# Attention and two expert layers on one core: one overflow loop instead of eight, three weight pieces ahead of it, attention's small work reordered

## The chip, the cores and the metric

One core of a Trainium2 chip runs the whole program. A core has five engines that run side by side, each with an instruction queue of its own that it works off in order: PE (matrix multiply; its weight loads are listed as PEld), DVE (vector), ACT (activation), POOL (general) and SP (which here only issues transfers). Transfers issued by SP, ACT and POOL are carried out by 16 DMA engines. Engines wait for each other by semaphores. The metric is the time of one execution in device microseconds.

## The reference

Inputs: q, k, v of 4 x 8 x 576 x 64 (batch, heads, positions, width), all float32, and weights. Three stages:

```
# attention: a coarse one on means of 4 positions, and a local one in a band of +-3 positions
q_d, k_d, v_d = mean over 4 positions of q, k, v
out  = repeat(softmax(q_d k_d^T / 8) v_d, 4) + softmax(band(q k^T / 8)) v
x    = out as (2304 tokens, 512)
# first expert layer: each token goes to one of 8 experts
e    = argmax(x w_gate);  scale = softmax(x w_gate)[e] * sigmoid(x w_output_gate)[e]
y    = scale * (relu(x w1[e]) w2[e])            # w1 (8, 512, 1024), w2 (8, 1024, 512)
# second layer, the same for all tokens
h    = y w_in;  result = (h * cos(h)) w_out     # 512 -> 2048 -> 512
```

## The kernel before

**Attention** (lines 116 to 770). The batches are two halves g of two, the heads four pairs hp: eight units (g, hp) of five items, two coarse (D) and three local (L), 40 items in all. `step(n)` (line 709) lays several items over each other in the order of the program: the scores of item n (`phase_a`, PE, then a maximum on DVE), the exponentials of item n - 1 (ACT) and their division (`phase_s`, two small operations on DVE and a multiplication on POOL, line 379), the transposes of item n - 2 (`phase_b`, PE, copied by ACT) and its product with V (`phase_c`, PE). Beside these stand, for the next unit, the transposes of q and k (`t_chunk`, PE, copied by DVE and ACT) and the sums of four positions (`sums`: q_sum on POOL, k_sum on DVE for units 0 and 1 and else on POOL, v_sum on DVE for unit 0 and else on POOL). SP loads q, k, v of unit u + 2 (`load`, `load_vr`) and the V windows of unit u + 1 (`load_vw`, rows of 70 positions whose unused partitions are zeroed once, lines 195 and 212). There are two V window buffers, `vw[0]` and `vw[1]`.

**The gate of the first half** becomes a list `bg` of small operations once the last tile of unit 3 is there (item 22): 18 operations on DVE, ACT and PE that choose the expert, rank the tokens (`rank`, PE) and give each its place, nine scales of 128 rows, and nine scatters (`scatter_one`, POOL: an indirect transfer of 128 scaled rows to the expert's region `xs` in DRAM). Between them goes `zero_count`, which finds the expert with the most rows so far (`leader`, five steps), and `zero_lead`. `flush(k)` (line 453) runs the list on by k units of cost (scale 2, scatter 4, else 1), twice an item with k = 4. From item 31 on (`early_step`) the weights of that leading expert are loaded, at item 36 its first 144 rows (`early_rows`), and after the items PE computes that expert for these rows. The second half's gate runs in three parts of three tiles behind the last items. `tables` (line 772) then sorts the experts by their number of rows and writes place, rows and the flag `over`: how many have more rows than the capacity CAPS of their place.

**The border** (lines 1097 to 1106). SP loads the first weight piece (`fetch(0)`), then the 408 rows of the largest expert (`load_rows(0)`), then the pieces s = 2 to 5. Then comes `overflow`: each engine loads `over` (line 843) and branches past the body (line 844) where it is 0. The body holds eight loops, one a place, each over that place's rows beyond its capacity in turns of 128; with its loop control it stands eight times in the program. Behind it `part(0)` splits piece 0 into a high and a low part (POOL and DVE), `x_tile(0, j)` transposes the rows (PE), with the high part by ACT and the low part by DVE, and `mm1(0)` needs both. A piece is 512 KB, five fit at a time.

**Experts and second layer** (to line 1266): PE runs matmuls in three passes back to back until the end. The order of all this is the order in which the program is written; there is no planner.

Of the kernel before, what the change touches and what calls it, by code (L numbers as in the profile page):

```python
# [18 lines left out]
NT = B * S  # L19
# [43 lines left out]
class Kernel:  # L63
# [54 lines left out]
    def attention(self, es):  # L118
# [76 lines left out]
        nc.vector.memset(vw[1][64:128], 0.0)  # L195
# [16 lines left out]
        nc.gpsimd.memset(vw[0][64:128], 0.0)  # L212
        nc.gpsimd.memset(vw[0][0:32, 0, 0, :], 0.0)
# [238 lines left out]

        def flush(k, stop=None):
            while bg and k > 0 and bg[0][1].__name__ != stop:
                f = bg.pop(0)[1]
                k -= COST.get(f.__name__, 1) if cur[0] < len(items) else 1
                f()

        def gating(g, i0, n):
# [70 lines left out]
            for t in range(n):  # L530
# [9 lines left out]
                (later if n == TG else scales).append(scatter_one)  # L540
# [168 lines left out]
        def step(n):  # L709
# [5 lines left out]
            if n - 1 in exps:  # L715
                exps.pop(n - 1)()
            if n < len(items):
                phase_a(n)
            evicts = []
# [8 lines left out]
            sums(n)  # L728
# [4 lines left out]
            if 0 <= n - 2 < len(items):  # L733
                phase_b(n - 2)
# [103 lines left out]
    def overflow(self, pool, psum, w1v, w2v):  # L838


        tc, nc = self.tc, self.nc
        ET = mybir.EngineType
        any_over = nc.values_load(self.over, min_val=0, max_val=NE)
        with tc.If(any_over > 0):
# [6 lines left out]
            for r in range(NE):  # L851
                c = CAPS[r]
                nr = nc.values_load(self.tab[0:1, 1, r:r + 1], min_val=0, max_val=NT)
                er = nc.values_load(self.tab[0:1, 0, r:r + 1], engines=[ET.SP], min_val=0, max_val=NE - 1)
                fr = nc.values_load(self.tab[0:1, 2, r:r + 1], engines=[ET.Pool], min_val=0, max_val=NT - EARLY)
                br = nc.values_load(self.tab[0:1, 3, r:r + 1], engines=[ET.SP, ET.Pool], min_val=0, max_val=NE * NT - 128)
                with tc.For_i(c, nr, 128) as i:
                    s = nc.s_assert_within(nr + (c - 128) - i, min_val=0, max_val=NT - 128)
                    col = nc.s_assert_within(fr + s + EARLY, min_val=0, max_val=NT - 128)
                    row = nc.s_assert_within(br + s, min_val=0, max_val=NE * NT - 128)  # L860
                    nc.sync.dma_start(out=x, in_=self.xs[bass.ds(row, 128), 0:DM])
                    for a in range(2):
# [20 lines left out]
    def experts(self, es):  # L883
# [215 lines left out]
        for s in range(2, NWR + 1):  # L1099
            fetch(s)  # L1100
# [181 lines left out]
```

## Time and profile before

| | |
|---|---|
| median of 3 runs | 862.24 us (858.41 to 863.38) |
| the profiled execution | 856.74 us, span 854.8 us from first to last instruction |
| PE busy | 805.5 us (94%), mean granted clock 0.983 |
| DVE, ACT, POOL busy | 525.5, 462.1, 210.6 us |
| attention and gates | to about 204 us of the span |
| experts (first layer) | 207.65 to about 440 us |
| second layer | from there to the end |

In the rows below a line of the timeline is: start in us, duration in us, engine, line of the kernel, operation, output <- inputs, shapes, count, and in brackets how long the engine sat idle before it and what ended that. A "q" behind an engine's name (PEldq, DVEq, SPq) means its sequencer: loads of registers, branches, semaphores and DMA issues. [...]

### The profile page before, as it was taken

To read this page: it belongs to the slowest core of one execution; us is meant where nothing else is said; L and a number is where in the kernel's file an instruction comes from. 1 tells how busy PE (TensorE), PEld (TensorE's weight loads), DVE (VectorE), ACT (ScalarE), POOL (GpSimd) and SP (SyncE) were. 2 spreads that over 40 slices of the span, in tenths; PEclk is the share of its full clock that TensorE was granted. 3 is DMA by queue.
4 is the path that set the end of the run, shared out by engine and by line. 5 is a ranking of instruction groups with operands and counts; after the bars stand their busy time and mean duration, and the time that the engine had idled before them with its cause. 6 is when DMAs were issued, how large, how long until landed. Compare 5 with 4: busy or idle time off the path is not lost.

```text
span 854.8 us, 15523 instructions
## 1 busy us (share of the span) xinstructions
PE 805.5 (94%) x5846; PEld 705.2 (83%) x5846; DVE 525.5 (61%) x952; ACT 462.1 (54%) x1105; POOL 210.6 (25%) x250
## 2 busy tenths in 40 slices
PE   6899987888999999999999989999999999999996
PEld 5778866777999999999986778888888888888895
DVE  4787886673579898997669883434343434343442
ACT  4679787642455655655456564445444444444453
POOL 5587758532000000000038751200020002000100
PEclk9999999989999999999999999999999999999998
DMA  7989959726758989998923320101010001000100
GB/s 150 177 197 235 249 121 252 172 102 229 259 174 221 251 271 237 253 286 251 279 71 99 99 74 1 50 0 50 1 50 0 25 1 46 4 1 1 50 1 25
DMA packets 86570, 107.15 MB, mean 125 GB/s; under 512 B 27837, under 2 KB 59613, under 8 KB 86487
## 3 DMA queue, kind: packets, MB, share of 16 engines
q1 hardware_dynamic: 79455, 85.94, 38.8%
q0 software_dynamic: 4432, 14.86, 4.9%
q10 hardware_dynamic: 2600, 5.27, 2.0%
q8 instruction: 48, 0.79, 0.4%
q14 instruction: 35, 0.29, 0.1%
HBM read 83.88 MB, written 22.19 MB: 124 GB/s over the span
## 4 chain that ended last, share of the span: by engine, by line
PE 60%; issue 7%; DVE 4%; ACT 2%; DMA 2%; POOL 0%; POOLq 0%; ACTq 0%; DVEq 0%; SPq 0%
PE hp L991 10%; PE hp L993 10%; PE hp L992 9%; PE op L993 6%; PE op L991 6%; PE op L992 6%; PE yp L991 4%; PE yp L993 4%; PE yp L992 4%; DMA raw<-in_moe_w_out_dram 2%; PE xp L983 1%; DVE tmp L1062 1%; DVE tmp L1063 1%; ACT w L919 1%; DMA yd<-st 0%
## 5 line engine op out<-in xcount | busy, mean ns | idle before, releaser
L1180 DVE SCALAR_TENSOR_TENSOR n<-n,hp 128x512 f32<-128x512 int32 (+1 forms) x80 | 50.6, 633 | 149.5 <-ACT n L1179 149.5
L1179 ACT ACTIVATE n<-hp 128x512 int32<-128x512 f32 (+1 forms) x80 | 44.3, 554 | 161.1 <-PE hp L993 158.3
L991 PE MATMUL hp<-yh,win 128*128 128x512 f32 (+1 forms) x320 | 118.8, 371 | 0.0
L993 PE MATMUL hp<-yh,win 128*128 128x512 f32 (+1 forms) x320 | 118.6, 371 | 0.0
L992 PE MATMUL hp<-yh,win 128*128 128x512 f32 (+1 forms) x320 | 117.9, 368 | 0.0
L993 PE MATMUL op<-w,g 128*128 128x512 f32 x288 | 114.2, 397 | 3.1 <-DVE g L920 3.0
L991 PE MATMUL op<-w,g 128*128 128x512 f32 x288 | 113.9, 396 | 2.2 <-ACT g L919 2.2
L992 PE MATMUL op<-w,g 128*128 128x512 f32 x288 | 113.7, 395 | 0.0
L1212 POOL DMA_INDIRECT out_dram<-o,ids_sb x18 | 18.7, 1038 | 310.1 <-DVE o L1210 306.2
L920 DVE TENSOR_TENSOR w<-wr,w 128x1024 fp32r<-128x1024 f32 x64 | 78.2, 1222 | 21.5 <-ACT w L919 16.5
L1187 DVE SCALAR_TENSOR_TENSOR n<-n,hp 128x512 f32<-128x512 f32 (+1 forms) x80 | 50.7, 633 | 52.9 <-ACT n L1186 52.9
L991 PE MATMUL yp<-h,w 128*128 128x408 f32 (+7 forms) x256 | 78.1, 305 | 2.5 <-DVE st L1027 2.4
L993 PE MATMUL yp<-h,w 128*128 128x408 f32 (+7 forms) x256 | 77.7, 303 | 0.0
L991 PE MATMUL hp<-xt,w 128*128 128x344 f32 (+7 forms) x252 | 77.6, 308 | 0.0
L992 PE MATMUL yp<-h,w 128*128 128x408 f32 (+7 forms) x256 | 77.6, 303 | 0.0
L993 PE MATMUL hp<-xt,w 128*128 128x344 f32 (+7 forms) x252 | 76.1, 302 | 0.0
L992 PE MATMUL hp<-xt,w 128*128 128x344 f32 (+7 forms) x252 | 76.0, 301 | 0.0
L1010 ACT ACTIVATE h<-hp 128x408 fp32r<-128x408 f32 (+7 forms) x64 | 27.2, 425 | 84.0 <-PE hp L993 81.1
L992 PEld LDWEIGHTS hp<-yh,win 128*128 128x128 f32 x320 | 60.6, 189 | 11.5
L991 PEld LDWEIGHTS hp<-yh,win 128*128 128x128 f32 x320 | 60.5, 189 | 11.0
L993 PEld LDWEIGHTS hp<-yh,win 128*128 128x128 f32 x320 | 60.4, 189 | 10.9
L993 PEld LDWEIGHTS op<-w,g 128*128 128x128 f32 x288 | 54.5, 189 | 17.9 <-DVE g L920 5.8
(207 smaller groups left out, 1797.7 us busy)
## 6 DMA issues: line engine op xcount, KB each, us to landing
wr<-in_moe_w_dram SPq DMA_DIRECT2D x64, 512.0 KB
raw<-in_moe_w_in_dram SPq DMA_DIRECT2D x16, 512.0 KB
raw<-in_moe_w_out_dram SPq DMA_DIRECT2D x16, 512.0 KB
xs<-zero ACTq DMA_DIRECT2D x8, 643.5 KB
rawq<-in_q_dram SPq DMA_DIRECT2D x16, 288.0 KB
rawk<-in_k_dram SPq DMA_DIRECT2D x16, 288.0 KB
rawv<-in_v_dram SPq DMA_DIRECT2D x16, 288.0 KB
vw<-in_v_dram SPq DMA_DIRECT2D x14, 315.0 KB
```

The lines of the kernel that those rows point to most:

```text
L919: nc.scalar.copy(out=w[:, 0], in_=src)
L920: (eng or nc.vector).tensor_tensor(out=w[:, 1], in0=src, in1=w[:, 0].bitcast(F32), op=ALU.subtract)
L983: nc.tensor.transpose(pt[:, k, 0:n], rows[r][0:n, j, 128 * k:128 * k + 128], ident[0:n, 0:n])
L991: nc.tensor.matmul(out=out, lhsT=wi(w[:, 0]), rhs=m[0], start=first, stop=False)
L992: nc.tensor.matmul(out=out, lhsT=wi(w[:, 0]), rhs=m[1], start=False, stop=False)
L993: nc.tensor.matmul(out=out, lhsT=wi(w[:, 1]), rhs=m[0], start=False, stop=last)
L1010: nc.scalar.activation(out=h[:, 0, 0:c], in_=hp[:, 0:c], func=AF.Relu)
L1062: V.tensor_scalar(out=t, in0=hi, scalar1=0x07FFFFFF, scalar2=3, op0=ALU.bitwise_and, op1=ALU.logical_shift_left)
L1179: nc.scalar.activation(out=m, in_=hp, func=AF.Copy, scale=0.15915494309189535)
L1180: nc.vector.scalar_tensor_tensor(out=m.bitcast(F32), in0=m, scalar=-6.283185307179586, in1=hp, op0=ALU.mult, op1=ALU.add)
L1187: nc.vector.scalar_tensor_tensor(out=a, in0=a, scalar=-1.0, in1=hp, op0=ALU.add, op1=ALU.mult)
L1212: ins = nc.gpsimd.indirect_dma_start(out=self.out[:, :], out_offset=bass.IndirectOffsetOnAxis(ap=ids[:, j:j + 1], axis=0), in_=o, in_offse ...
```

## The change

Four things. The memsets of the two V window buffers swap engines. In the first half's gate a `flush` runs at most one scatter an item, starts `rank` only at the head of a flush, and has four of the nine scatters among the scales; this holds until the second half's gate begins. In the first unit, `sums` of items 0 and 1 goes ahead of their scores, and `phase_b` ahead of the transposes of the next unit. In the experts, three pieces are loaded ahead of the rows, two behind `overflow`, and `overflow` has a single loop: DVE computes the rows beyond the capacities of all eight places, adds up the turns, and in each turn takes the place with most rows left. The computation of a turn is the same (cut below).

```diff
--- before.py
+++ after.py
@@ -192,7 +192,8 @@
 
         load(0)
 
-        nc.vector.memset(vw[1][64:128], 0.0)
+        nc.vector.memset(vw[0][64:128], 0.0)
+        nc.vector.memset(vw[0][0:32, 0, 0, :], 0.0)
 
         for h in range(2):
             m = band[64 * h:64 * h + 64]
@@ -209,8 +210,7 @@
             nc.gpsimd.memset(kt2[i][:, PAD + 2 * S:], 0.0)
         for t in pl2:
             nc.gpsimd.memset(t[:, :, KW:128], 0.0)
-        nc.gpsimd.memset(vw[0][64:128], 0.0)
-        nc.gpsimd.memset(vw[0][0:32, 0, 0, :], 0.0)
+        nc.gpsimd.memset(vw[1][64:128], 0.0)
         load_vw(0)
         load_vr(0)
         load(1)
@@ -450,8 +450,19 @@
             else:
                 nc.vector.tensor_tensor(out=acc, in0=acc, in1=lv, op=ALU.add)
 
+        sent = set()
+
         def flush(k, stop=None):
+
+
+            k0 = k
             while bg and k > 0 and bg[0][1].__name__ != stop:
+                if len(gates) < 2:
+                    nm = bg[0][1].__name__
+                    if nm == "scatter_one" and cur[0] in sent or nm == "rank" and k < k0:
+                        break
+                    if nm == "scatter_one":
+                        sent.add(cur[0])
                 f = bg.pop(0)[1]
                 k -= COST.get(f.__name__, 1) if cur[0] < len(items) else 1
                 f()
@@ -537,7 +548,13 @@
                 scales.append(scale)
                 def scatter_one(t=t):
                     scatter(t)
-                (later if n == TG else scales).append(scatter_one)
+                if n < TG:
+                    scales.append(scatter_one)
+                else:
+
+                    later.append(scatter_one)
+                    if t % 2:
+                        scales.append(later.pop(0))
             if t0 + n == NTILE:
 
                 tp = ps_o.tile([128, 512], F32, tag="o", name="o_ps")
@@ -714,8 +731,12 @@
             u, slot = divmod(n, 5)
             if n - 1 in exps:
                 exps.pop(n - 1)()
+            if n < 2:
+                sums(n)
             if n < len(items):
                 phase_a(n)
+            if not u and n >= 2:
+                phase_b(n - 2)
             evicts = []
             if n < len(items) and u + 1 < len(units):
                 if slot == (LS if u else 3) and u + 2 < len(units):
@@ -725,12 +746,13 @@
                     load_vw(u + 1)
                 for c in {0: (0, 1), 1: (2, 3), 2: (4, 5)}.get(slot - (0 if u else 2), ()):
                     evicts.append(t_chunk(u + 1, c))
-            sums(n)
+            if n >= 2:
+                sums(n)
             if 0 <= n - 1 < len(items):
                 phase_s(n - 1)
             for e in evicts:
                 e(1)
-            if 0 <= n - 2 < len(items):
+            if u and n - 2 < len(items):
                 phase_b(n - 2)
             for e in evicts:
                 e(0)
@@ -838,8 +860,10 @@
     def overflow(self, pool, psum, w1v, w2v):
 
 
-        tc, nc = self.tc, self.nc
+
+        tc, nc, V = self.tc, self.nc, self.nc.vector
         ET = mybir.EngineType
+        MOST = NT // 128
         any_over = nc.values_load(self.over, min_val=0, max_val=NE)
         with tc.If(any_over > 0):
             w1s = [pool.tile([128, 2, F1], F32, tag="win", name="v_w1", bufs=8) for _ in range(2)]
@@ -848,37 +872,60 @@
             h = pool.tile([128, 8, 128], F32, tag="win", name="v_h", bufs=8)
             x, xt, yt = xr[:, 0], xr[:, 1].rearrange("p (k n) -> p k n", k=4), xr[:, 2].rearrange("p (k n) -> p k n", k=4)
             ps = [psum.tile([128, 4, 128], F32, tag=f"y{d}", name="yp") for d in range(4)]
-            for r in range(NE):
-                c = CAPS[r]
-                nr = nc.values_load(self.tab[0:1, 1, r:r + 1], min_val=0, max_val=NT)
-                er = nc.values_load(self.tab[0:1, 0, r:r + 1], engines=[ET.SP], min_val=0, max_val=NE - 1)
-                fr = nc.values_load(self.tab[0:1, 2, r:r + 1], engines=[ET.Pool], min_val=0, max_val=NT - EARLY)
-                br = nc.values_load(self.tab[0:1, 3, r:r + 1], engines=[ET.SP, ET.Pool], min_val=0, max_val=NE * NT - 128)
-                with tc.For_i(c, nr, 128) as i:
-                    s = nc.s_assert_within(nr + (c - 128) - i, min_val=0, max_val=NT - 128)
-                    col = nc.s_assert_within(fr + s + EARLY, min_val=0, max_val=NT - 128)
-                    row = nc.s_assert_within(br + s, min_val=0, max_val=NE * NT - 128)
...
+            tab, caps = self.tab, self.caps
+            small = pool.tile([1, 2048], F32, tag="win", name="v_s", bufs=8)
+            left, key, sel, io = (small[:, 8 * j:8 * j + 8] for j in range(4))
+            top = small[:, 32:33]
+            prod = small[:, 64:88].rearrange("p (a e) -> p a e", a=3)
+            steps = small[:, 128:128 + MOST]
+            many = small[:, 256:256 + NE * MOST].rearrange("p (e j) -> p e j", j=MOST)
+            now = small[:, 1024:1027].bitcast(I32)
+            turns = small[:, 1032:1033].bitcast(I32)
+            nc.gpsimd.iota(io, pattern=[[1, NE]], base=0, channel_multiplier=0, allow_small_or_imprecise_dtypes=True)
+            nc.gpsimd.iota(steps, pattern=[[128, MOST]], base=0, channel_multiplier=0, allow_small_or_imprecise_dtypes=True)
+            V.tensor_tensor(out=left, in0=tab[:, 1, :], in1=caps, op=ALU.subtract)
+            V.tensor_tensor(out=many, in0=left.unsqueeze(2).to_broadcast([1, NE, MOST]),
+                            in1=steps.unsqueeze(1).to_broadcast([1, NE, MOST]), op=ALU.is_gt)
+            with nc.allow_low_precision(reason="whole numbers, added in float32"):
+                V.tensor_reduce(out=turns, in_=small[:, 256:256 + NE * MOST], axis=AX.X, op=ALU.add)
+            n_turns = nc.values_load(turns, min_val=0, max_val=MOST + NE)
+            with tc.For_i(0, n_turns, 1):
+                V.scalar_tensor_tensor(out=key, in0=left, scalar=float(NE), in1=io, op0=ALU.mult, op1=ALU.add)
+                V.tensor_reduce(out=top, in_=key, axis=AX.X, op=ALU.max)
+                V.tensor_tensor(out=sel, in0=key, in1=top.to_broadcast([1, NE]), op=ALU.is_equal)
+
+                V.scalar_tensor_tensor(out=key, in0=left, scalar=-128.0, in1=caps, op0=ALU.add, op1=ALU.add)
+                V.tensor_copy(out=prod[:, 0, :], in_=tab[:, 0, :])
+                V.tensor_tensor(out=prod[:, 1, :], in0=tab[:, 2, :], in1=key, op=ALU.add)
+                V.tensor_tensor(out=prod[:, 2, :], in0=tab[:, 3, :], in1=key, op=ALU.add)
+                V.tensor_tensor(out=prod, in0=prod, in1=sel.unsqueeze(1).to_broadcast([1, 3, NE]), op=ALU.mult)
+                with nc.allow_low_precision(reason="whole numbers, added in float32"):
+                    V.tensor_reduce(out=now, in_=prod, axis=AX.X, op=ALU.add)
+                V.scalar_tensor_tensor(out=left, in0=sel, scalar=-128.0, in1=left, op0=ALU.mult, op1=ALU.add)
+                er = nc.values_load(now[0:1, 0:1], engines=[ET.SP], min_val=0, max_val=NE - 1)
+                col = nc.values_load(now[0:1, 1:2], engines=[ET.Pool], min_val=0, max_val=NT - EARLY - 128) + EARLY
+                row = nc.values_load(now[0:1, 2:3], engines=[ET.SP, ET.Pool], min_val=0, max_val=NE * NT - 128)
+                nc.sync.dma_start(out=x, in_=self.xs[bass.ds(row, 128), 0:DM])
+                for a in range(2):
+                    nc.sync.dma_start(out=w1s[a], in_=w1v[bass.ds(er, 1), :, 2 * a:2 * a + 2, :].rearrange("e p k f -> p (e k) f"))
+                    nc.sync.dma_start(out=w2s[a], in_=w2v[bass.ds(er, 1), :, 4 * a:4 * a + 4, :].rearrange("e p c d -> p (e c) d"))
+                nc.gpsimd.dma_start(out=self.ids[bass.ds(col, 128), :],
+                                    in_=self.xs[bass.ds(row, 128), DM:DM + 1].bitcast(I32))
...
+                nc.vector.tensor_copy(out=yt, in_=ps[3])
+                nc.gpsimd.dma_start(out=self.ydv[:, :, bass.ds(col, 128)], in_=yt)
 
     def experts(self, es):
         tc, nc = self.tc, self.nc
@@ -1094,11 +1141,13 @@
                     wout.append(pool.tile([128, 2, 2, DM], F32R, tag="w", name="w", bufs=NW if pool is outer else 8 - NW))
                 split(wout[j // 2][:, :, j % 2, :], t, nc.gpsimd)
 
-        fetch(0)
+        for s in (0, 2, 3):
+            fetch(s)
         load_rows(0)
-        for s in range(2, NWR + 1):
+
+        self.overflow(outer, ps_y, w1v, w2v)
+        for s in range(4, NWR + 1):
             fetch(s)
-        self.overflow(outer, ps_y, w1v, w2v)
         part(0)
         for j in range(4):
             x_tile(0, j)
```

## Rows read from the trace of the kernel before

**Rows 1.** busy us (counts) of PE, PEld, DVE, ACT, POOL; PEclk, DMA, GB/s
```profile
55.90:90.90 35.00, 34.03 (x557) 29.25 (x556) 27.43 (x70) 30.57 (x130) 26.75 (x36) 1.00 0.88 216
98.40:117.20 18.80, 15.51 (x214) 12.71 (x212) 15.32 (x46) 13.14 (x58) 11.81 (x15) 0.91 0.92 226
117.20:158.70 41.50, 33.55 (x495) 28.44 (x495) 29.52 (x80) 31.03 (x122) 31.29 (x37) 0.92 0.75 215
...
208.00:210.00 2.00, 2.00 (x11) 2.00 (x10) 0.90 (x1) 0.96 (x2) 0.00 (x0) 0.50 0.92 305
```

**Rows 2.** timeline of PE and one SP issue, from 16 to 177 us
```profile
16.10 1.70 PE L331 MATMUL s_ps<-kd,qd 64*64 64x144 f32 x12 [2.40 <-DVE kd L307]
...
22.81 1.30 PE L251 MATMUL ptq<-ident,rawq 128*128 128x128 f32 x5 [1.60 <-DMA rawq<-in_q_dram]
...
26.61 0.96 PE L351 MATMUL s_ps<-kt,qt 64*64 64x70 f32 x24
...
33.58 0.88 PE L390 MATMUL ptpd<-ident,pd 128*128 128x128 f32 x6 [1.55 <-POOL pd L379]
...
111.06 0.72 PE L411 MATMUL o_ps<-ptd,vd 128*64 128x144 f32 x8 [0.95 <-DVE cum L522]
...
117.21 0.96 PE L351 MATMUL s_ps<-kt,qt 64*64 64x70 f32 x24 [0.44 <-DVE vals L572]
...
142.10 1.33 PE L400 MATMUL ptpl<-ident,pl 128*128 128x128 f32 x6 [1.99 <-POOL pl L379]
...
158.72 0.96 PE L351 MATMUL s_ps<-kt,qt 64*64 64x70 f32 x24
...
161.09 0.88 SPq L616 DMA_DIRECT2D ea_rows<-xs  x2
...
177.04 1.65 PE L645 MATMUL ptx<-ident,ea_rows 128*128 128x128 f32 x8
```

**Rows 3.** timeline of POOL: memset, rawv of unit 1, a second scatter
```profile
6.77 2.02 POOL L212 MEMSET vw<- 64x2304 f32 x1
...
30.11 2.55 POOL L288 TENSOR_TENSOR dv<-rawv 72x512 f32<-72x512 f32 x2 [4.92 <-DMA rawv<-in_v_dram]
...
143.52 0.96 POOL L495 DMA_INDIRECT xs<-xsb,g_pi  x1 [0.30 <-PE ptpl L400]
```

**Rows 4.** SP's waits: us in total, times, longest
```profile
SPq L184 <- POOL vw L213: 5.2, 1, 5.2
```

**Rows 5.** DMA share from 4 to 9 us, tenths in 40 slices
```profile
DMA  9998999997999899999899797974510000000000
```

**Rows 6.** timeline at the border, all engines
```profile
196.45 0.38 SPq L947 DMA_DIRECT2D wr<-in_moe_w_dram  x1
...
199.98 4.08 PE L661 MATMUL ea_y<-mask,ea_rawv 128*128 128x144 f32 x32
...
201.58 1.46 SPq L967 DMA_DIRECT2D rows<-xs  x3
...
207.65 3.24 PE L983 MATMUL xp<-ident,rows 128*128 128x128 f32 x16 [3.59 <-PEq L844]
...
209.10 1.23 DVE L920 TENSOR_TENSOR w<-wr,w 128x1024 fp32r<-128x1024 f32 x1 [4.94 <-DMA wr<-in_moe_w_dram]
```

**Rows 7.** GB/s from 201 to 204 us in 40 slices
```profile
GB/s 0 0 0 0 0 0 0 0 0 0 0 0 0 0 0 0 0 0 0 0 27 137 109 55 109 164 382 382 382 355 355 328 355 383 382 382 410 410 410 410
```

**Rows 8.** line 844, the branch, by sequencer: ns, first and last start
```profile
L844 ACTq EVENT_SEMAPHORE  x2: 17/17/17, 205.2 to 205.2; - x2
...
L844 DVEq EVENT_SEMAPHORE  x2: 21/21/21, 208.7 to 208.8; - x2
...
L844 PEldq COMPARE_BRANCH  x1: 5032/5032/5032, 202.3 to 202.3; - x1
L844 DVEq COMPARE_BRANCH  x1: 72/72/72, 204.5 to 204.5; - x1
L844 ACTq COMPARE_BRANCH  x1: 45/45/45, 204.7 to 204.7; - x1
```

More of the change, by code (lines that the diff above doesn't have):

```diff
@@ new lines, in overflow @@
+            with nc.allow_low_precision(reason="whole numbers, added in float32"):
[22 more added lines that the diff above has]
+                                    in_=self.xs[bass.ds(row, 128), DM:DM + 1].bitcast(I32))
+                for k in range(4):
+                    nc.tensor.transpose(ps[0][:, k, :], x[:, 128 * k:128 * k + 128], self.ident)
+                nc.vector.tensor_copy(out=xt, in_=ps[0])
+                for f in range(8):
+                    for k in range(4):
+                        nc.tensor.matmul(out=ps[1 + f // 4][:, f % 4, :], lhsT=w1s[k // 2][:, k % 2, 128 * f:128 * f + 128],
+                                         rhs=xt[:, k, :], start=(k == 0), stop=(k == 3))
+                for a in range(2):
+                    nc.scalar.activation(out=h[:, 4 * a:4 * a + 4, :], in_=ps[1 + a], func=AF.Relu)
+                for d in range(4):
+                    for f in range(8):
+                        nc.tensor.matmul(out=ps[3][:, d, :], lhsT=w2s[f // 4][:, f % 4, 128 * d:128 * d + 128],
+                                         rhs=h[:, f, :], start=(f == 0), stop=(f == 7))
+                nc.vector.tensor_copy(out=yt, in_=ps[3])
+                nc.gpsimd.dma_start(out=self.ydv[:, :, bass.ds(col, 128)], in_=yt)
```

19 lines of the change are left out of this document (removed).

## The prediction

> **What bounds the kernel now.** I read the page first: 94% of the span is PE, and from 214 us to the end the chain of waits is a row of PE matmuls back to back. The change touches nothing there, so whatever it gains or loses must come before 214 us and is then carried to the end one for one. I next read the sums of busy time by stretch [rows 1]. From 55.90 to 90.90 us PE is busy 34.03 of 35.00: this is attention at its own pace. Ten items go through there (n = 10 to 19), so 3.5 us an item. From 98.40 to 117.20 the gates of the first half lie among four items, which take 18.80 us instead of 14.0; from 117.20 to 158.70 scales and scatters lie among nine items, which take 41.50 instead of 31.5. PE has holes there and the clock is under 1.00. Then the order on PE, its waits and SP's issue of the early rows [rows 2], POOL's order [rows 3], SP's wait and the transfers at the start [rows 4, 5], and the border between attention and experts [rows 6 to 8].
>
> The capacities are not exceeded with these inputs: the trace holds no instruction of the body at lines 867 to 881. What the new loop costs when it runs plays no part; what counts is how an engine gets past it.
>
> **The change part by part.**
>
> **(A) Start: V window, sums and phase_b.** SP's V load of unit 0 waits 5.2 us for POOL's memset [rows 4]: it comes at 6.77 us, behind the masks [rows 3]. The change gives it (2.02 us, and a small one) to DVE, which does the other window's today as its first work; POOL takes that one at the old place, and item 3 is the first to want it. SP thus issues the V loads and unit 1's loads some 5 us earlier, right behind q and k of unit 0. That doesn't give 5.2 us: the DMA strip from 4 to 9 us [rows 5] shows the engines full until about 8.0 us with q and k of unit 0, on the same SP queue, so V can only use the hole from there to where its packets move today, some 1.3 us after SP goes on at 9.0: 2.3 us. Two reads hang on that stream: PE's at 22.81 us (rawq of unit 1, 1.60 us waited [rows 2]) and POOL's at 30.11 us (rawv, 4.92 us waited [rows 3]). The other edits remove waits of PE: k_sum runs in DVE's hole ahead of the mask add, so the scores at 16.10 us (2.40 us waited for it) come earlier, and phase_b of item 0 goes ahead of the transposes that wait for rawq. Item 3 (26.61 us) then starts some 3.5 us earlier. But at item 4 phase_b goes ahead too, and there PE waited for POOL until 33.58 us [rows 2], after five transposes that now stand behind that wait: POOL's product comes 2.3 us earlier with its data, and the transposes and their evictions follow it, which gives back about 1 us. I take -1.5 us. Bounds: -5.2 (the whole wait goes) and +1.5 (PE's wait of 1.55 us at item 4 stays and everything behind it is late).
>
> **(B) The gates of the first half.** No operation goes or comes. Rank moves from the second flush of item 24 to the head of the first flush of item 25 and stops the flush until then; place, the zero count, its leader steps and the scales follow one item later. Of the 4.8 us lost here, one wait names its cause: PE 0.95 us for DVE's cum behind rank [rows 2]. That goes; DVE's list of small operations stays. I take -1.0, bounds -4.8 and +1.0 (the delayed list meets a full DVE one item later).
>
> **(C) One scatter an item.** Counting through the list: now the nine scatters go two each at items 28 to 31 and one at 32, after four scales at item 27 alone. After it, one each at items 26 to 34, with at most two scales beside it. A scatter costs POOL 0.96 us, and 0.30 us of idle before a second [rows 3]: 1.3 us. POOL is in order, and the multiplication of the item's probabilities, for which PE's transposes wait, stands behind sums and scatters: PE waits 1.99 us at 142.10 [rows 2], again 1.99 us ten us later, and both times the clock falls. What would POOL need if nothing else stopped it? In the 41.50 us it was busy 31.29 [rows 1]; with 9 x 0.30 that is 34.0 us, and 5% for waits between engines makes 35.8. PE with 33.55 us, some of it at half clock, DVE with 29.52 and ACT with 31.03 stand below it. So -5.7 us. Bounds: nothing, if POOL's waits move elsewhere, and -10.0 (PE's pace, 9 x 3.5). The other side, +5.2, is in the rivals. The last scatter goes from item 32 to 34. Behind it on SP stand the read of the early rows (item 36) and two weight pieces; SP issues that read at 161.09 us and PE uses the rows at 177.04 [rows 2], the pieces later still, so two items of delay, about 7 us, stay hidden.
>
> **(D) The border.** PE's last early matmul ends at 204.06 us, the first transpose of the experts starts at 207.65: 3.59 us idle, put down to the branch [rows 6]. By sequencer [rows 8]: PE's branch took 5.03 us from 202.3; DVE's took 0.07, but its next instruction came at 208.7, 4.1 us later; ACT's next one came 0.5 us after its branch (204.7). DVE then does part(0) from 209.10 and the four low halves of xt, until 212.28. The 16 transposes run until 210.9, in part at clock 0.50 [rows 1]. After it the body is once there, not eight times: about 300 instead of 2389 instructions on PE and some 50 instead of 272 on DVE, counted in the compiled program. I take ACT's 0.5 us for each engine, since it is the row of a short skip. PE is then ready before 204.06, and DVE at 205.0. What is late next? The rows. They are issued at 201.58, when the last scatter has landed; that stays. The two pieces now ahead of them are issued right behind fetch(0) at 196.45, their places being free as fetch(0)'s is, and put 1.05 MB before the rows on SP's queue. The DMA strip shows 0 GB/s for the first 1.5 us from 201 us, then 330 to 410 GB/s [rows 7]. At 380 the two pieces take 2.8 us, 1.5 of them in that hole: rows about 1.3 us later, all in by about 206.5. The transposes follow them, the second group of hp starts about 208.5 instead of 212.34. I take -3.5. Bounds: -5.5 (idle and half clock both go), and +3.0 (1.05 MB at 234 GB/s, 4.5 us, on rows that land at 206). Of the five pieces issued before the branch today, two (s = 4 and 5) now go behind SP's load of the flag and its branch; PE wants them after the first three only.
>
> [...] The rows don't bear out that distance decides alone: ACT and DVE skip 271 and 272 instructions, one loses 0.5 us and the other 4.1.
>
> **Sum.** -1.5 - 1.0 - 5.7 - 3.5 = -11.7 us. The profiled execution took 856.74 us (span 854.8), so 845.0. The median of the runs is 862.24, 5.5 us above it; the same difference gives **850.5**.
>
> **The rivals.**
>
> (1) The branch still misses its target on PE or DVE. Speaks for it that DVE lost 4.1 us where ACT lost 0.5 over the same distance. With either engine late, the other's gain is worth nothing, since the second group of hp needs both: D = -0.4, the time 862.24 - 8.6 = 853.6.
>
> (2) Attention gives nothing back: ACT or DVE, each over 29 us in the 41.5, takes POOL's place as soon as scales and gates overlap otherwise. Against it: the continuous row on POOL at items 28 to 32 (two scatters behind each other in each), and scales that are now spread too. With A, B and C at 0 and D = -3.5: 858.7.
>
> (3) Slower: transfers, not engines, set the pace. Place: the 16 DMA engines from 117 to 159 us (share 0.75) and at the border (0.92) [rows 1]. If a scatter's rows wait for those engines, items 28 to 32 stay as long as they are, and items 26, 27, 33 and 34 each get 1.3 us more on POOL: C = +5.2; at the border the rows fall behind 1.05 MB: D = +3.0. With A and B at -2.5 the time is 862.24 + 5.7 = 867.9. It decides from the point where C and D together exceed 2.5. Against it: the waits name no transfer that POOL waits for among the scatters of items 28 to 32.
>
> (4) The edits do nothing that can be seen, 862.2: attention's stalls go to other waits and the branch keeps its cost.
>
> **How the numbers follow.** Forecast 0.58, (1) 0.18, (2) 0.10, (3) 0.09, (4) 0.05. 0.5% (4.3 us) is what a measurement of this kernel tells from no change, so faster is below 857.9. The forecast's own range is 843 to 857, (1) lies below 857.9 in nearly all its width: faster 0.75 of these two. (2) and (4) are the same: 0.15, with a little of (1). Slower: 0.10. The low end comes from C and D near their bounds (862.24 - 1.5 - 1 - 10 - 5.5 = 844) with a little of A and B; the high end takes in (2). I give 842 to 860.
>
> **What would show it.** A: the V loads issue near 4 us and item 3's scores start near 23 us. B: no wait for cum behind rank. C: one scatter between two multiplications on POOL, no wait of 2 us for them on PE, and items 26 to 35 in about 36 us. D: the sequencers of PE and DVE go on within a us of their branches, rows come before PE's transposes by little or after them, and the clock row at the border stays near 1.00. The prediction is wrong if POOL's multiplications still come late with one scatter an item, if PE's branch still takes 5 us, or if the stretch behind 214 us changes its length.

## The result, and the profile after

The changed kernel takes 854.19 us (median of 14 runs, one disturbed run at 1559.83 counted in it, 853.41 without it; the others 850.16 to 857.17), the kernel before 862.22 in the same comparison: ratio 0.9904, 95% interval 0.9885 to 0.9922. By the two medians that is 8.0 us less, by the ratio 8.3 (6.7 to 9.9), where 11.7 were forecast.

The two profiled executions don't show this: before's took 856.74 us, less than any of its 14 timed runs, after's took 857.17, the top of the range of its own. What follows goes by landmarks that recur in all profiles: the start of an item's scores on PE, the end of the early matmuls (the leading expert's, for its first 144 rows), the start of the first three-pass matmul (behind the first 12 expert matmuls). Behind that last one, 13 of the 14 profiles of this study have 639.8 to 641.9 us to the end of the span (before: 854.8 - 213.93 = 640.9). Only after's own has 644.6, because its first load of y came late (used 14.6 us behind its issue, 11.2 us in before's profile). The change did not alter that stretch; executions differ there. The piece of its chain of waits (start, us, what):

```profile
416.54 14.58 DMA y<-yd
```

| landmark | before | after |
|---|---|---|
| item 3, 5, 22 starts | 26.61, 35.72, 98.38 | 23.37, 33.63, 96.09 |
| item 26, 35, 39 starts | 117.21, 158.72, 171.48 | 114.03, 152.37, 165.13 |
| early matmuls end | 204.06 | 200.43 |
| first three-pass matmul | 213.93 | 211.14 |

PE's timeline after, with the places that answer to [rows 2] and [rows 6] (start, duration, instruction, idle before and its releaser):

```profile
23.37 1.67 PE L351 MATMUL s_ps<-kt,qt 64*64 64x70 f32 x24
...
114.03 0.96 PE L351 MATMUL s_ps<-kt,qt 64*64 64x70 f32 x24 [2.19 <-DVE vals L589]
...
122.44 0.86 PE L440 MATMUL ptx<-ident,xt 128*128 128x128 f32 x3 [2.01 <-DVE xt L429]
...
203.47 3.04 PE L1030 MATMUL xp<-ident,rows 128*128 128x128 f32 x16 [3.03 <-SPq L868]
206.92 4.42 PE L1051 MATMUL hp<-xt,w 128*128 128x408 f32 x12 [0.42 <-ACT xt L966]
211.14 0.42 PE L1038 MATMUL hp<-xt,w 128*128 128x408 f32 x1
```

Item 3 is 3.2 us ahead, item 22 still 2.3, items 35 and 39 6.4. From there to the end of the early matmuls this execution loses 2.7 us of the lead, in code that the change leaves as it was. The windows of that stretch (busy of PE, PEld, DVE, ACT, POOL; granted clock, which is PEclk, the share of its full clock that PE was granted; DMA share, GB/s), before and after:

```profile
171.48:204.06 32.58, 29.60 (x312) 27.18 (x311) 18.78 (x86) 10.75 (x47) 11.59 (x12) 0.90 0.36 129
165.13:200.43 35.30, 32.37 (x313) 29.58 (x311) 18.88 (x88) 10.76 (x47) 12.21 (x13) 0.81 0.52 138
```

PE is idle for 3.0 and 2.9 us; what differs for PE is the clock, 0.90 and 0.81. The run with early rows below, whose code is the same there, took 32.60 us at 0.90. So this loss is the execution's and not the change's.

The two waits of 1.99 us for POOL's multiplications have gone (the longest left is 1.38 us, at 130.67). Two waits for DVE, 0.44 us at item 26 [rows 2] and 1.40 us at item 27, have grown to 2.19 and 2.01. At the border PE still waits 3.03 us. The releaser's name there is the sequencer's, but line 868 by engine says that the branch no longer holds anyone; it answers to [rows 8]:

```profile
L868 PEldq COMPARE_BRANCH  x1: 353/353/353, 198.7 to 198.7; - x1
L868 DVEq COMPARE_BRANCH  x1: 72/72/72, 200.9 to 200.9; - x1
L868 ACTq COMPARE_BRANCH  x1: 45/45/45, 201.0 to 201.0; - x1
L868 DVEq EVENT_SEMAPHORE  x2: 21/21/21, 201.4 to 201.6; - x2
```

PE's branch takes 0.35 us in place of 5.03, DVE goes on 0.5 us behind its own in place of 4.1. What PE waits for is the rows: the timeline of POOL and SP shows the last scatter, and 5.3 us behind it, with a wait of SP for that scatter's transfer, the issue of the rows, which PE gets 4.24 us later. Then the windows of the border (columns as above), which answer to [rows 1]:

```profile
193.91 0.96 POOL L506 DMA_INDIRECT xs<-xsb,g_pi  x1 [0.30 <-issue]
199.23 1.44 SPq L1014 DMA_DIRECT2D rows<-xs  x3
```

```profile
200.00:205.00 5.00, 1.95 (x13) 1.27 (x12) 1.76 (x4) 1.13 (x3) 0.83 (x1) 0.95 0.89 314
205.00:210.00 5.00, 4.58 (x18) 4.08 (x18) 3.29 (x5) 2.32 (x4) 0.00 (x0) 0.50 0.96 309
```

Behind PE's idle the granted clock is 0.50 in the whole second window, and the first 12 expert matmuls take 0.37 us each (4.42 us together), where they took 0.20 at a granted clock of 1.00 (2.45 us together, in the run with early rows below).

### The profile page after: what moved, and what is told of

Read it like the earlier page. It is cut to its first block, busy times and chain, and to the rows that moved or that the text cites. A ratio compares the mean times of both kernels' runs of the same rounds, so it can differ in the third digit from the quotient of the medians.

```text
span 855.7 us, 15524 instructions
## 1 busy us (share of the span) xinstructions
PE 806.9 (94%) x5846; PEld 707.9 (83%) x5846; DVE 531.4 (62%) x953; ACT 462.0 (54%) x1105; POOL 210.5 (25%) x249
## 4 chain that ended last, share of the span: by engine, by line
PE 58%; issue 6%; DVE 4%; DMA 4%; ACT 2%; POOL 0%; POOLq 0%; ACTq 0%; DVEq 0%; SPq 0%
PE hp L1038 9%; PE hp L1040 9%; PE hp L1039 9%; PE op L1040 6%; PE op L1038 6%; PE op L1039 6%; PE yp L1038 4%; PE yp L1040 4%; PE yp L1039 3%; DMA raw<-in_moe_w_out_dram 2%; DMA y<-yd 2%; PE xp L1030 1%; DVE tmp L1109 1%; DVE tmp L1110 1%; DVE w L967 1%
## 5 line engine op out<-in xcount | busy, mean ns | idle before, releaser
L1038 PE MATMUL yp<-h,w 128*128 128x408 f32 (+7 forms) x256 | 79.1, 309 | 2.6 <-DVE st L1074 2.4
L1040 PE MATMUL yp<-h,w 128*128 128x408 f32 (+7 forms) x256 | 78.9, 308 | 0.8 <-DVE w L967 0.8
L1039 PE MATMUL yp<-h,w 128*128 128x408 f32 (+7 forms) x256 | 78.6, 307 | 1.1 <-DVE h L1058 1.1
L1039 PEld LDWEIGHTS hp<-yh,win 128*128 128x128 f32 x320 | 60.7, 190 | 11.5
```

Of the source, the lines that this page charges most:

```text
L1038: nc.tensor.matmul(out=out, lhsT=wi(w[:, 0]), rhs=m[0], start=first, stop=False)
L1039: nc.tensor.matmul(out=out, lhsT=wi(w[:, 0]), rhs=m[1], start=False, stop=False)
L1040: nc.tensor.matmul(out=out, lhsT=wi(w[:, 1]), rhs=m[0], start=False, stop=last)
```

## The experiments

**Which part earns it?** Attention alone, and the border alone, each on the kernel before.

```
e1_attention: after.py's attention + before.py's overflow() and experts()
e2_border:    before.py's attention + after.py's overflow() and experts()
```

> The kernel before with the attention part of the change alone (the swapped zero fills, the reordered step, one scatter an item); the border is the one of before, with its branch over 2,389 PE instructions. Theory (the gain is the attention's, the border gave nothing): item 35 starts near 152.4 us as in the changed kernel (before: 158.7), the time is 854 us, within 1 us of the changed kernel's 854.2. Rival (the border gave most of it, what attention gains is given back on the way): 859 to 860 us, 2 to 3 below the kernel before.

> The kernel before with the border part alone: the one loop over turns, and three pieces fetched ahead of the rows. Theory (the branch's 5 us go, but PE then waits for the rows, and a longer stretch at half clock follows): PE's branch falls from 5.0 to 0.4 us, PE waits about 3 us for the rows, the stretch from the end of the early matmuls to the first three-pass matmul stays at 9.3 to 10.7 us (before: 9.87), the time 861.5 to 863 us. Rival (the border is worth the 3.5 us of the forecast): the stretch is 6.4 us, the time 858 to 859 us.

Measured on one chip (before 863.02): attention alone 853.02, ratio 0.9894 (0.9865 to 0.9923), that is 9.1 us less; the border alone 861.9, ratio 0.9999 (0.9978 to 1.0021). The theory holds, the rival falls. In the border run PE's branch took 0.35 us, PE waited 3.12 us for the rows, and the stretch from the early matmuls to the first three-pass one was 11.8 us, 1.1 over the range named. With the old border beside the new attention PE waited 2.15 us, for its branch by name; but the branch ended at 200.31 us, and PE's weight load at 200.60 had waited 2.34 us for the rows by name, so the rows were as late as the branch.

**Do the two pieces ahead hold up the rows?**

```diff
-        for s in (0, 2, 3):
-            fetch(s)
+        fetch(0)
         load_rows(0)
         self.overflow(outer, ps_y, w1v, w2v)
-        for s in range(4, NWR + 1):
+        for s in range(2, NWR + 1):
```

> The changed kernel with the order of fetches of the kernel before: one piece ahead of the rows, then the branch, then the other four. Theory (the 1 MB of the two pieces ahead holds up the rows): the rows are issued at the same distance behind the last scatter (5.3 us) but PE's first transpose comes 1.5 to 2 us sooner, 2.2 to 2.7 us behind the first rows' issue in place of 4.2; the time 852 to 853 us. Rival (4.2 us is what rows take anyway): PE's first transpose does not move, and the two pieces that come later cost 0 to 1.5 us: 854 to 856 us.

853.33 us, ratio 0.9904 (0.9872 to 0.9936), the same as with the pieces ahead. PE's transposes here name the rows as what they wait for:

```profile
202.48 1.76 PE L1030 MATMUL xp<-ident,rows 128*128 128x128 f32 x8 [2.18 <-DMA rows<-xs]
205.38 1.64 PE L1030 MATMUL xp<-ident,rows 128*128 128x128 f32 x8 [1.13 <-DMA rows<-xs]
```

The first ones did come sooner, 3.66 us behind the rows' issue in place of 4.24 (the theory had named 1.5 to 2 us of gain), but the third block of rows then came late, and the first three-pass matmul stood 11.3 us behind the early ones in place of 10.7. The pieces ahead neither cost nor give. This run is also the one loop beside the new attention on the chip where attention alone, with its eight loops, took 853.02: the one loop gives nothing there either.

**Why did the scatters' stretch give less than forecast?** With one scatter an item, the first two fall among the leader's steps. DVE (first four) and POOL of the changed kernel there:

```profile
118.45 1.95 DVE L843 TENSOR_TENSOR ahead<-vals,t_lead 1x8 f32<-1x8 f32 x1
120.43 0.62 DVE L844 TENSOR_TENSOR ahead<-ahead,io 1x8 f32<-1x8 f32 x1
121.08 0.15 DVE L845 TENSOR_REDUCE t_lead<-ahead 1x1 f32<-1x8 f32 x1
...
124.88 1.41 DVE L849 TENSOR_SCALAR ahead<-ahead 1x8 f32<-1x8 f32 x1
```

```profile
117.87 1.19 POOL L506 DMA_INDIRECT xs<-xsb,g_pi  x1 [0.17 <-issue]
119.09 1.28 POOL L290 TENSOR_TENSOR vd<-dv 72x512 f32<-72x512 f32 x1
120.31 0.71 POOL L296 TENSOR_TENSOR dq<-qt 128x288 f32<-128x288 f32 x1
...
125.44 0.83 POOL L306 TENSOR_TENSOR dt<-kt 128x288 f32<-128x288 f32 x1
```

Operations on eight numbers that take 0.15, 0.15 and 0.41 us in before's profile take 1.95, 0.62 and 1.41 us, and each ends within 0.04 us of a POOL operation's end (120.37, 121.02, 126.27); the reduction beside them is not stretched (0.15 us). So each stretched operation ends with one of POOL's; what stretches it, these rows do not show. The run held the first scatters back until the steps were through:

```diff
             bg.insert(12, (0, zero_lead))
+            at = max(i for i, x in enumerate(bg) if x[1].__name__ in ("most", "first", "row", "one", "rest"))
+            hold = [x for x in bg[:at] if x[1].__name__ == "scatter_one"]
+            bg[:] = [x for x in bg[:at + 1] if x not in hold] + hold + bg[at + 1:]
```

> The changed kernel, with the first scatters held back until the leader's steps on DVE are through. Theory (DVE's tiny steps from and to SBUF stand still while POOL scatters or adds; three of them took 1.95, 0.62 and 1.41 us in place of 0.15 to 0.41): the steps take 0.15 us again, items 27 to 28 take 4.2 to 5 us in place of 6.9, item 35 starts 2 to 2.5 us sooner, the time 851.5 to 852.5 us. Rival (POOL's own list is the limit, and the two scatters put off are paid in items 30 to 36): item 35 starts within 0.7 us of 152.4, the time 853.5 to 855 us.

851.36 us, ratio 0.9876 (0.9848 to 0.9904): 2.0 below the run with the rows first on that chip, with overlapping intervals. Items 27 to 28 took 5.48 us, not 4.2, and items 26 to 35 37.59 in place of 38.34: 0.8 us, not 2.5. The first of these is a poor measure, since three profiles without this edit (attention alone and the two with early rows below) took 4.2 us there. The second came again in three of four later profiles with this edit (37.6 us), but not in the fourth (38.58, at a clock of 0.92). The theory is right about the stretched steps and a third right about what they cost: some steps still stretch beside POOL's sums and the first scatter (line 846 0.68 us, line 857 0.74, line 858 0.78), and the pace from item 30 on is POOL's (in the changed kernel's profile it is busy for 18.33 of the 19.56 us from item 30 to 35).

**The clock, the rows and the branch at the border.** Three runs:

```
e5_busy_border:          the kernel of the run above, 20 matmuls of 128 columns between overflow and the transposes
e6_rows_free:            the changed kernel, load_rows(0) reads rows of w2 instead of xs
e7_rows_free_old_border: the kernel of attention alone, load_rows(0) likewise
```

The last two leave out the first place's true rows and do not compute the reference.

> The kernel with the leader's steps clear of the scatters (851.4 us), with 20 more PE matmuls of 128 columns behind the branch, whose result nobody reads, so that PE is busy while it waits for the rows. Theory (the half clock behind the border comes from PE's idle 3 us; the first 12 expert matmuls took 0.37 us each in place of 0.19): the granted clock stays near 1.00 from 200 to 210 us, the first three-pass matmul comes 1.5 to 2.2 us sooner behind the early matmuls (11.1 us there), the time 849 to 850 us. Rival (the clock falls all the same, or falls later instead): 851 to 852 us.

> The changed kernel, but the first place's rows are read from a weight input, so that they don't wait for the scatters (the first place's rows are not the reference's). Theory (behind the one-loop branch the border waits for the rows, whose chain starts at the last scatter): PE's first transpose comes within 0.8 us of the end of the early matmuls in place of 3.0, the first expert matmul 4 to 4.5 us behind it in place of 6.5, the time 850.5 to 852 us. Rival (something else is next: the cast of the first piece, the clock): the border shortens by under 1 us, 853.3 to 854.3 us.

> The attention part alone with the border of before (853.0 us), and the first place's rows read from a weight input as well, so that only the branch is left to wait for (the first place's rows are not the reference's). Theory (PE's skip over 2,389 instructions is hidden by the rows' chain, and costs as soon as the rows are early): PE still waits 2 to 3.6 us for its branch, the time 852 to 853 us, 1.5 to 2.5 above the one-loop kernel with early rows. Rival (the branch costs PE nothing there either): the time is within 0.7 us of the one-loop kernel with early rows.

On one chip (before 858.96, 3 to 4 us less than on the chips that the expected times were taken from): 850.68 us, ratio 0.9909 (0.9886 to 0.9931); 846.28, 0.9862 (0.9839 to 0.9886); 854.79, 0.9954 (0.9938 to 0.9971). PE's timeline at the border of the second, then of the third:

```profile
198.50 2.46 PE L1031 MATMUL xp<-ident,rows 128*128 128x128 f32 x16 [1.11 <-SPq L868]
201.52 2.45 PE L1052 MATMUL hp<-xt,w 128*128 128x408 f32 x12 [0.56 <-ACT xt L966]
203.81 0.35 PE L1039 MATMUL hp<-xt,w 128*128 128x408 f32 x1
```

```profile
203.46 3.34 PE L1006 MATMUL xp<-ident,rows 128*128 128x128 f32 x16 [5.03 <-PEq L866]
207.22 4.42 PE L1027 MATMUL hp<-xt,w 128*128 128x408 f32 x12 [0.42 <-ACT xt L941]
211.44 0.54 PE L1014 MATMUL hp<-xt,w 128*128 128x408 f32 x1
```

With early rows the one loop leaves PE idle for 1.11 us (the rows were still late: a weight load at 199.25 waits 0.33 us for them by name), the granted clock is 1.00 from 200 to 205 us, the first expert matmul comes 4.1 us behind the early ones (end 197.39), as the theory said, and the first three-pass matmul 6.4 us. With the eight loops PE waits 5.03 us, the granted clock is 0.50 from 205 to 210 us, and the first three-pass matmul comes 13.0 us behind (end 198.43). The times are 8.5 us apart, of which these two profiles show 6.6 at the border. So the branch has its price, and in the changed kernel it is covered by the rows. For the third run the theory expected 2 to 3.6 us of wait and 1.5 to 2.5 us of time, and was too low. The 20 matmuls of the first run did keep the clock: it was 1.00 from 195 to 210 us, and the 12 matmuls took 2.62 us. But they lasted 4.70 us, longer than the 3.1 us of idle, so the transposes began 4.8 us behind the early matmuls; the first three-pass matmul came 1.3 us sooner (9.8 us behind), under the theory's 1.5 to 2.2, and no gain shows in the time. Fewer of them were not tried.

**The start alone, and the rule alone.**

```
e8_start_only:        before.py + memset swap + order of sums and phase_b in step()
e12_scatter_rule_only: before.py + flush() with `sent` and rank's rule + the order of scatters in gating()
```

> The kernel before with the start of the attention part alone: the swapped zero fills and the reordered first steps; not the rule of one scatter an item, not the border. Theory (the start is worth its 2.3 us, and they last): items 5 to 25 start 2.1 to 2.3 us sooner than before (n=20 at 88.6 in place of 90.9), the time 859.5 to 861 us; the other 6 of the attention part are then the rule on scatters and rank. Rival (the start's lead is given back where POOL sets the pace, items 30 to 34): item 35 starts within 1 us of before's 158.7, the time 861.5 to 863 us.

> The kernel before with the rule on scatters and rank alone (one scatter an item, rank at the head of a turn); not the swapped zero fills, not the reordered start, not the border. Theory (the rule is the main part of the attention's gain, and needs nothing of the start): items 22 to 26 take 0.9 us less than before's 18.8, items 26 to 35 3.2 less than its 41.5, the time 5 to 8 us below before. Rival (its gain hangs on the start's shift, or shrinks as the transfers collide): under 3 us below before.

The start alone: 860.0 us, ratio 1.0011 (0.9997 to 1.0026), no gain (same chip as the three runs above, before 858.96). The rule alone, on another chip (before 862.51): 856.76, ratio 0.9945 (0.9922 to 0.9967), 4.7 us less by the ratio and 5.8 by the medians, where 5 to 8 were named; items 26 to 35 took 38.31 us, as expected, items 22 to 26 18.30, where 17.9 were. Where the start's lead goes is in the window 30 to 35 us and the wait in it: the start alone first, then the changed kernel.

```profile
30.00:35.00 5.00, 3.63 (x23) 3.31 (x24) 1.76 (x4) 2.04 (x6) 4.54 (x6) 0.50 0.96 196
```

```profile
30.00:35.00 5.00, 4.06 (x62) 3.62 (x63) 3.39 (x10) 4.17 (x20) 4.15 (x6) 1.00 0.95 190
```

```profile
31.37 1.54 PE L390 MATMUL ptpd<-ident,pd 128*128 128x128 f32 x6 [3.79 <-POOL pd L379]
```

Item 4 starts at 26.62 us there (before: 30.37), PE then waits 3.79 us for POOL's product, whose data has just come (POOL's sum of rawv starts at 27.90), and works at a granted clock of 0.50 behind it: item 5 starts at 36.36, behind before's 35.72. Eleven profiles have the new start. In six the clock is 1.00 in that window and item 5 starts between 33.3 and 34.2; in five it is 0.5 to 0.66 and item 5 starts between 35.1 and 36.4. The five are those in which item 4 started earliest (25.9 to 26.9 us, the six 27.4 to 28.4): PE came sooner to the wait for POOL, stood idle longer (2.97 to 3.79 us, in the six 1.75 to 2.30), and worked at that lower clock behind it. The same run lost more at the first pair of scatters: items 26 to 35 took 45.99 us (116.12 to 162.11), because POOL stood 4.42 us ahead of the first scatter, for nothing that the profile names, and PE behind it.

```profile
134.88 1.18 POOL L495 DMA_INDIRECT xs<-xsb,g_pi  x1 [4.42 <-issue]
136.37 0.97 POOL L495 DMA_INDIRECT xs<-xsb,g_pi  x1 [0.30 <-issue]
```

```profile
139.53 1.54 PE L400 MATMUL ptpl<-ident,pl 128*128 128x128 f32 x6 [5.22 <-POOL pl L379]
```

Without the rule two scatters follow each other there with a multiplication behind both; with it the first one stands alone two items earlier. For the time the rival was nearly right: it had put this run between 0.7 us below and 0.8 above before, and it took 1.0 more than before on its chip (860.0 as a bare number lies in the theory's range, but before was 3.3 us faster on this chip). On the place it was right that the lead goes at POOL, but item 35 started 3.4 us behind before's, not within 1.

**Can the rows be had earlier?** Three runs on the kernel with the leader's steps clear. The early rows' matmuls that stood among the last items go behind the last rank; the scales and scatters of the last group go ahead of the table's steps; and the first of these with the old border.

```diff
-EB, EA = {1: 1, 2: 1, 3: 1}, {2: 2, 3: 1, 4: 16}
+EB, EA = {}, {4: 16}
```

> The kernel with the leader's steps clear of the scatters (10.6 us below the kernel before, in its own comparison), and the four up matmul groups of the early rows that stood among the last attention items put behind the last rank instead. Theory (the border waits for the rows, whose chain runs from the last gating through the last scatter; work of PE behind that gating hides it): the last scatter comes 3 to 5 us sooner before the end of the early matmuls, PE's wait for the rows falls from 3.1 to under 1 us, the first three-pass matmul comes 6.5 to 9 us behind the early matmuls in place of 11.1; 13 to 15.5 us below before. Rival (those groups filled waits of PE that now stay empty, and the end of the early matmuls comes later by as much): 10 to 11 us below before.

> As the run with the up groups last, and the last group's scales and scatters go ahead of the table's steps on DVE instead of between them. Theory (each us of the scatter chain is a us of the border as long as PE waits for rows): the last scatter 0.5 to 1 us sooner, 0.3 to 1 us less than the run with the up groups last. Rival (rows come early enough by then, or the later table holds up the first fetch): the same within 0.5 us, or up to 1 more.

> As the run with the up groups last, but with the border of the kernel before (eight loops, one piece ahead of the rows). Theory (the one loop is worth the branch's time once the rows are early, as with the rows from a weight input, where it was 8 us): PE waits 4 to 5 us for its branch, the time 4 to 8 us above the run with the up groups last. Rival (the skip stays hidden): within 1.5 us of it.

On one chip (before 862.51): 852.97 us, ratio 0.9881 (0.985 to 0.9913); 852.21, 0.9866 (0.9834 to 0.9898); 861.49, 0.9991 (0.9969 to 1.0012). PE at the border, of the first and the third:

```profile
203.79 1.85 PE L1033 MATMUL xp<-ident,rows 128*128 128x128 f32 x16 [0.30 <-PEq L871]
```

```profile
211.17 3.27 PE L1008 MATMUL xp<-ident,rows 128*128 128x128 f32 x16 [4.34 <-PEq L869]
```

The wait for the rows is gone, and so is the clock of 0.50 (1.00 from 205 to 210 us, the 12 matmuls take 0.97 and 1.74 us): the first three-pass matmul stands 6.3 us behind the early ones (11.1 without the edit). But those come 38.7 us behind item 39 in place of 33.0, since PE idles among the last items where the moved matmuls had been (1.85 us ahead of the last rank). Item 39 to the first three-pass matmul is 44.96 us with the edit, 44.09 without: the rival was right on the time. The theory was right on the branch: the same order with eight loops is 8.5 us slower, and PE waits 4.34 us for a branch of 5.77 us. Of the 8.5 the two profiles show 4.1 at the border (10.3 us against 6.3); the rest lies in stretches that the two kernels share and is not put down to a place. The second run, with the table last, is within the noise of the first (44.34 us for the same stretch). The lowest ratios of kernels that compute the reference are these 0.9866 and the 0.9876 with the leader's steps clear, against 0.9904 for the changed kernel; the intervals overlap and the chips differ, so a version that beats it is likely but not shown.

## Why the prediction was right, and where it was not

The direction, the range and the place of the largest part were right; the sum was -11.7 and came out at -8.0, and the parts were not what the sum said.

**(A), -1.5.** The V loads issue at 3.79 us, item 3 starts at 23.37: as said. What is left of it depends on PE's clock at the wait for POOL at item 4, which the prediction kept as its other bound: 1.5 to 2.4 us at item 5 in six profiles, -0.6 to +0.6 in five, and no gain in time when alone, on one chip.

**(B), -1.0.** The pair gives 18.83 to 17.94, as forecast, and the wait for cum is gone; 2.19 us for DVE's copy of the zero count stand in its place. The windows of these four items, after and with the start alone (which has not the rule, and still waits 0.95 us for cum):

```profile
96.09:114.03 17.94, 14.03 (x216) 11.47 (x212) 15.39 (x46) 13.01 (x58) 11.83 (x15) 1.00 0.96 220
98.21:116.12 17.91, 13.96 (x216) 11.39 (x213) 15.60 (x46) 13.17 (x58) 11.83 (x15) 1.00 0.93 217
```

PE's idle time did not fall (3.3 us before, 3.9 after); the clock was 0.91 before and 1.00 after, and at 1.00 the same 17.9 us came without the rule. Three kernels without it took 18.8, 19.3 and 17.9 us at 0.91, 0.82 and 1.00, eleven with it 17.9 to 18.3 at 0.90 to 1.00. So the rule may give a part of the 0.9 us, but that the number came out as forecast is in part luck.

**(C), -5.7.** The mechanism was right and the size was not: 41.5, 41.6 and 46.0 us without the rule, 38.3 to 38.8 with it in six profiles, so some 3.2 where no other wait comes in. The term that was mis-sized is POOL's own list plus 5% (the 5% was the author's estimate): items 30 to 34 do follow it at 3.9 us each, but items 26 to 30 take 4.7 each. DVE was nearly full there (9.51 of 10 us from 120 to 130), and DVE's small steps stretched beside POOL's scatters and sums (to 1.95 us in place of 0.15). Of 2.5 us missing, holding the scatters back gave 0.8 in four of five profiles; that the rest has the same cause is not shown.

**(D), -3.5.** Here the step "rows about 1.3 us later, all in by about 206.5" failed, together with "the clock row at the border stays near 1.00". The branch went as forecast, on PE and on DVE, though with some luck: ACT's 0.5 us, from which its price was taken, is what two of the six profiles with eight loops show, and the other four have 3.6 to 4.9. The rows came too late. 206.5 is 2.4 us behind the end of the early matmuls; by the completions in the traces, the four transfers of rows landed 3.0 to 4.5 us behind it after (203.42 to 204.93), and already 0.15 to 3.45 us behind it before (204.21 to 207.51). PE idled 3.03 us in place of 3.59. The granted clock was then 0.50 (from 205 to 210 us) through 12 matmuls (4.4 us where before's profile shows 2.7). Nor is that tied to the one loop: of ten profiles with at least 2 us of idle here, eight took 4.1 to 4.5 us, four of these with eight loops. The two that took 2.7 and 2.5 (before, and the old border with the up groups last) had idles of 3.59 and 4.34, so the length of the idle does not tell it either. From the early matmuls to the first three-pass one, four profiles with eight loops have 9.9, 12.1, 11.5 and 10.4 us (before, attention alone, start alone, rule alone), four with one loop 10.7, 11.8, 11.3 and 11.1: no gain. Rival (1) had the right size for the wrong reason: PE's branch fell to 0.35 us and DVE went on 0.5 us behind its own, but the rows took the branch's place. No run shows its -0.4 for the border apart from the rest; the pair of profiles shows +0.8 there (9.9 before, 10.7 after). Rival (3) fell: the scatters' stretch got shorter, and the order of the pieces changed nothing.

**What is left.** By the ratios the rule alone makes 4.7 us, the start alone -1.0, both together 9.1 (6.6 to 11.6). These come from three chips, on which before took 862.51, 858.96 and 863.02, so it is not shown that the parts help each other. One profile speaks for it: without the rule the start's lead went at the first scatters (45.99 us); without the start the rule keeps its 3.2. The landmarks give 6.4 us at item 35. About 2 us of the 8.0 are not put down to a place: the landmarks are those of one execution of each kernel, before's shorter than any of its timed runs and quick at the border too (12 matmuls in 2.7 us), after's the longest in the range of its own. Why POOL stood 4.42 us ahead of its first scatter with the start alone stays open.

## What to carry to other kernels

Before an edit removes a wait, take the next releaser's own chain back to its start. Here the first rows landed 3.1 us ahead of the branch's end in before's profile, but in the two profiles with the rule on scatters and eight loops PE still waits for rows by name behind it (0.72 us with attention alone, 0.58 with the rule alone). So the edit that removed the branch gave nothing until runs with early rows laid its price bare, 4 to 7 us at the border and 8.5 in time. PE's idle of 3.03 us ahead of the experts cost more than itself here, because the granted clock was 0.50 behind it (12 matmuls in 4.4 us in place of 2.5), so a half-removed wait can be worth nothing. A profile is one execution: compare the stretches of several kernels that share the code before a difference of 1 or 2 us is believed.

## What the runs showed of the hardware

- A skip over 2,389 PE instructions took between 3.59 and 6.47 us in six profiles of the old border (5.03 in [rows 8]; 3.59 with attention alone, 6.47 with the rows read early); no run separates what sets it. With the one loop it took 0.35 us in four (the changed kernel, the border alone, the rows read early, the up groups last). PE's sequencer reaches the branch some 1.7 us before the last early matmul ends (202.3 to 204.06 before, 198.7 to 200.43 after), and that much is hidden.
- On DVE and ACT the skip of some 270 instructions cost 4.1 and 0.5 us in before's profile and 3.3 and 3.7 with attention alone; over the six profiles DVE has 2.8 to 5.9, ACT 0.5 in two and 3.6 to 4.9 in four. For those two the distance does not tell the price.
- DVE's operations on one row of eight numbers took up to 1.95 us in place of 0.15 while POOL scattered or added (changed kernel, line 843; line 821 before).
- The rows that wait for the last scatter were issued 3.7 to 6.3 us after that scatter's start (eleven profiles), though POOL itself is done with it in 0.96 us.
